# A fused state-space convolution and gated linear unit: kept weights, smaller transform units, one DMA per token load or store, and a spectrum swap by DMA

## The chip, the cores and the metric

The kernel runs on one core of a Trainium2 chip. The metric is device microseconds (us) of one execution, as the median of several. Executions of one kernel mostly agree within 1 to 1.5%; the kernel before had one outlier of 512.8 us, which no ratio uses. "Span" is the time from the first to the last instruction of the profiled execution and is about 2 us shorter than the time of that same execution.

The profiled execution is a single one. For the kernel before it took 281.01 us, 3.6 above the median; in the profiles of b_2q and b_one_stores, which change its stores alone, PE ends at 264.5 and 265.0 us where the profile of before has 266.8. So some 2 us of what this profile loses probably belong to that execution, and a difference of 2 us between two profiles is not safe by itself.

The engines, as the profile names them: PE (matrix multiplies) with PEld (its weight loads), DVE (vector engine), ACT (scalar engine), POOL, and SP, which here only issues DMA transfers. ACT issues some too (four of the token loads of before stand in its queue on the page). The order of each engine's instructions is fixed when the kernel is built. PSUM is where the kernel's matrix multiplies write; an evacuation is a copy of a result out of it, by ACT or DVE (1.01 and 1.22 us for one of 128x1024, on the page of before), and PE's next work in that slot stands behind it.

## The reference

Two branches are added to a residual. Sequence 2048, width 640, hidden width 1728; everything is bf16.

```python
def conv(q, k, v, shift_k, ssm_k, ssm_D):
    kv = shift4(k, shift_k) * v                    # four-tap shift along the sequence
    y  = irfft(rfft(pad(kv)) * rfft(pad(ssm_k)))   # long convolution, length 4096
    return q * (y[:2048] + kv * ssm_D)

def glu(x, w_gate, w_up, w_down):
    return (sigmoid(x @ w_gate) * (x @ w_up)) @ w_down

# The residual stream is q; glu runs on its layernorm. Output: 1 x 2048 x 640.
```

## The kernel before

The kernel computes both branches side by side. The gated linear unit runs over four blocks of 512 tokens: gate and up products, sigmoid times up, then the down product. The convolution runs in ten sub-blocks (five for each half of the channels). A sub-block has a first transform, a second transform, complex products on DVE, and a third transform; each half ends with a fourth transform. PSUM slots called "g" serve the linear unit, and two slots "c" the convolution. A table of numbers in the source fixes the order of all pieces of work on all engines. It was computed offline, so nothing moves when a transfer comes late.

The parts that the change touches, as they were:

```python
# token row = (n q m): partition p = 32*q + n, 16 tokens m for each partition
xq4 = A_q.flatten_outer_dims().rearrange("(n q m) d -> q n m d", q=4, m=NQ)
oq4 = out.flatten_outer_dims().rearrange("(n q m) d -> q n m d", q=4, m=NQ)

def load_x(q, m0, m1, eng, pri):                      # called for q = 0, 1, 2, 3
    dma(lambda e: e.dma_start(acc[32 * q:32 * q + 32, m0:m1, :], xq4[q][:, m0:m1, :]), ...)

def store(m0, m1, pri, two=False):                    # 8:12, 0:8, 12:14, 14, 15
    for q in range(4):
        dma(lambda e, q=q: e.dma_start(oq4[q][:, m0:m1, :], acc[32 * q:32 * q + 32, m0:m1, :]), ...,
            q="ACT" if two and q % 2 else "SP", ...)

# second transform: two units of 64 matmuls, each filling both "c" slots
for i in range(2):
    ...
    pe(1060, 64, f, ..., alloc=[(c, "c") for c in cs] ...)

# products of a sub-block: four multiplies of 64 partitions, then two of 128
for h in range(2):
    for b in range(2):
        a, o = slice(64 * h, 64 * h + 64), slice(64 - 64 * h, 128 - 64 * h)
        dve(..., nc.vector.tensor_tensor(Q(b)[a], X(b)[a], H(b)[o], ALU.mult), ...)
for b in range(2):
    dve(..., nc.vector.tensor_tensor(X(b), X(b), H(b), ALU.mult), ...)

# gate and up: sigmoid on ACT, product with the up half straight from PSUM on DVE
act(512, lambda: nc.scalar.activation(tl[sg][:], tl[cs[0]][:], ACT.Sigmoid), ...)
dve(512, 1, lambda: nc.vector.tensor_tensor(hT[:, fc, :], tl[sg][:], tl[cs[1]][:], ALU.mult), ...)
```

## Time and profile before

| | before |
|---|---|
| timed median | 277.43 us (first three runs), 276.8 to 278.0 us in the later sessions |
| profiled span | 279.1 us |
| PE busy / DVE / ACT | 252.7 / 207.0 / 144.0 us |
| PE's last work ends | 266.8 us |
| tail behind it | 12.3 us |

How to read it: the first line of the page gives each engine's busy time. The rows of 40 digits are slices of the span in tenths busy; PEclk is the granted clock in tenths. The chain is the sequence of work that ended last, followed backwards. The prediction below shows these lines for the kernel before.

### The profile page before, as it was taken

Reading aid. Unit: us, or ns where it says so; the run is one execution under the profiler, and the core shown is the slowest. Engines: PE = TensorE matmul, PEld = TensorE weight load, DVE = VectorE, ACT = ScalarE, POOL = GpSimd, SP = SyncE. Lnnn points to the kernel's source line nnn. Section 1 sums busy time; section 2 is a strip of 40 time slices with the busy share of each in tenths; the row PEclk is TensorE's granted clock in tenths of the full one; section 3 lists DMA queues with packets and bytes.
Section 4 is the critical chain, followed back from the end, with each engine's and each line's share of the span. In section 5 each row is a group of like instructions: output and inputs, shape, how many; then the busy total and the mean of one; then the engine's idle time right before and its main releaser. Section 6 shows DMA issues by size and latency. Waiting matters only on the chain.

```text
span 279.1 us, 9682 instructions
## 1 busy us (share of the span) xinstructions
PE 252.7 (91%) x4344; PEld 156.5 (56%) x4380; DVE 207.0 (74%) x342; ACT 144.0 (52%) x214; POOL 0.7 (0%) x6
## 2 busy tenths in 40 slices
PE   8899887997799999999999999999999999999800
PEld 3754334774355547777456646667655555776500
DVE  5433147899489998869979998999888568864840
ACT  4642586133699979436557654224457754341100
POOL 1000000000000000000000000000000000000000
PEclk9999997999799999999999999999999999999965
DMA  7999999999769984999987602900464110000266
GB/s 181 265 234 290 193 202 192 152 273 256 148 132 338 193 218 115 166 216 152 250 168 209 162 2 67 295 25 5 116 194 167 44 31 2 2 2 2 63 132 188
DMA packets 94720, 42.17 MB, mean 151 GB/s; under 512 B 68432, under 2 KB 93592, under 8 KB 94360
## 3 DMA queue, kind: packets, MB, share of 16 engines
q1 hardware_dynamic: 94488, 41.24, 65.5%
q8 instruction: 34, 0.56, 0.9%
q10 hardware_dynamic: 192, 0.33, 0.4%
q14 instruction: 6, 0.05, 0.1%
HBM read 35.00 MB, written 5.24 MB: 144 GB/s over the span
## 4 chain that ended last, share of the span: by engine, by line
PE 83%; issue 4%; ACT 3%; DMA 3%; DVE 2%; SPq 1%; DVEq 0%; ACTq 0%
PE g L730 34%; PE g L745 23%; PE c L514 8%; PE c L582 4%; PE c L493 3%; PE c L552 3%; PE c L551 3%; DMA acc<-in_A_q_dram 3%; PE g L775 2%; PE g L710 2%; ACT jk L615 1%; ACT jk L621 1%; ACT xnT L312 1%; SPq L366 0%; DVE xq L652 0%
## 5 line engine op out<-in xcount | busy, mean ns | idle before, releaser
L730 PE MATMUL g<-xnT,w 128*128 128x512 bf16 x484 | 116.3, 384 | 4.6 <-issue 2.1
L730 PEld LDWEIGHTS <-w 128*128 128x128 bf16 x520 | 48.5, 99 | 56.8 <-issue 3.3
L745 PE MATMUL g<-wd,hT 128*128 128x320 bf16 x448 | 67.7, 304 | 0.1
L698 DVE TENSOR_TENSOR hT<-sig,g 128x512 bf16<-128x512 bf16 x52 | 35.4, 687 | 25.8 <-PE g L730 17.8
L745 PEld LDWEIGHTS <-hT 128*128 128x128 bf16 x448 | 42.4, 99 | 17.3 <-issue 0.4
L696 ACT ACTIVATE sig<-g 128x512 bf16<-128x512 f32 x52 | 30.8, 596 | 27.8 <-PE g L730 26.1
L312 ACT CAST S<-c 128x1024 bf16<-128x1024 f32 x25 | 24.8, 1012 | 21.8 <-PE c L514 21.8
L536 DVE TENSOR_TENSOR P<-S 64x1024 bf16<-64x1024 bf16 x40 | 27.4, 686 | 8.2 <-PE c L552 3.7
L514 PEld LDWEIGHTS <-Mt 64*128 64x128 f16 x1280 | 19.9, 95 | 10.5 <-issue 9.3
L312 ACT CAST V<-c 128x1024 bf16<-128x1024 f32 x20 | 19.4, 1013 | 11.5 <-PE c L552 11.5
L514 PE MATMUL c<-T,Mt 64*128 64x64 bf16 x1280 | 22.3, 190 | 2.9 <-issue 2.9
L313 DVE CAST S<-c 128x1024 bf16<-128x1024 f32 x15 | 18.3, 1223 | 5.5 <-PE c L514 5.4
L315 ACT ACTIVATE T<-c 128x1024 bf16<-128x1024 f32 x14 | 13.9, 1022 | 15.6 <-PE c L493 15.6
L551 PE MATMUL c<-At,S 128*128 128x128 f16 x160 | 19.3, 219 | 0.0
L552 PE MATMUL c<-At,P 128*128 128x128 f16 x160 | 19.3, 219 | 0.0
L312 ACT CAST T<-c 128x1024 bf16<-128x1024 f32 x14 | 13.8, 1014 | 10.6 <-PE c L493 10.5
L551 PEld LDWEIGHTS <-S 128*128 128x128 bf16 x160 | 15.6, 98 | 1.3 <-DVE S L539 0.2
L552 PEld LDWEIGHTS <-P 128*128 128x128 bf16 x160 | 15.6, 98 | 1.2
L756 DVE TENSOR_TENSOR acc<-g,acc 128x320 bf16<-128x320 f32 x32 | 14.5, 485 | 0.9 <-PE g L745 0.7
L458 DVE TENSOR_TENSOR tb<-kt,sT 128x1024 bf16<-128x1024 bf16 x20 | 13.7, 687 | 0.7 <-ACT kt L312 0.6
L463 DVE TENSOR_TENSOR ta<-ta,tb 128x1024 bf16<-128x1024 bf16 x20 | 13.8, 688 | 0.3
L539 DVE TENSOR_TENSOR S<-S 128x1024 bf16<-128x1024 bf16 x20 | 13.1, 688 | 0.3
(76 smaller groups left out, 196.1 us busy)
## 6 DMA issues: line engine op xcount, KB each, us to landing
w<-in_B_w_gate_dram SPq DMA_DIRECT2D x11, 640.0 KB, 4.8
w<-in_B_w_up_dram SPq DMA_DIRECT2D x11, 640.0 KB, 6.8
kt<-in_A_k_dram SPq DMA_DIRECT2D x8, 320.0 KB, 7.6
vt<-in_A_v_dram SPq DMA_DIRECT2D x8, 320.0 KB, 7.1
xnd<-xq SPq DMA_DIRECT2D x4, 640.0 KB, 7.5
ht<-in_A_ssm_k_dram SPq DMA_DIRECT2D x16, 96.0 KB, 6.3
wd<-in_B_w_down_dram SPq DMA_DIRECT2D x3, 480.0 KB, 5.5
acc<-in_A_q_dram SPq DMA_DIRECT2D x4, 320.0 KB, 7.3
```

The costliest lines, as they stand in the source:

```text
L312: fa = lambda: nc.scalar.copy(out=out_fn(), in_=in_fn())
L313: fd = lambda: nc.vector.tensor_copy(out_fn(), in_fn())
L315: fa = lambda: nc.scalar.activation(out_fn(), in_fn(), ACT.Copy, scale=scale)
L514: nc.tensor.matmul(tl[cs[e]][:, b, 64 * kk:64 * kk + 64], lhsT=Mb[rows, k, 64 - 64 * r:192 - 64 * r], rhs=tl[T][rows, 2 * k + r].rearrange ...
L536: dve(n, 2, lambda a=a, o=o, b=b: nc.vector.tensor_tensor(Q(b)[a], X(b)[a], H(b)[o], ALU.mult), r=sr + ([(Z, b, 0)] if h else []), w=[(Z, ...
L551: nc.tensor.matmul(o, lhsT=tl[S_][:, b, 0, j, :], rhs=Ab[:, 0, :], start=True, stop=False)
L552: nc.tensor.matmul(o, lhsT=tl[Z][:, b, j, :], rhs=Ab[:, 1, :], start=False, stop=True)
L696: act(512, lambda: nc.scalar.activation(tl[sg][:], tl[cs[0]][:], ACT.Sigmoid), r=[(cs[0],)], w=[(sg,)], alloc=[(sg, "sig")], pri=pri - 2000)
L698: dve(512, 1, lambda: nc.vector.tensor_tensor(hT[:, fc, :], tl[sg][:], tl[cs[1]][:], ALU.mult), r=[(cs[1],), (sg,)], w=[(hk, fc)], pri=pri ...
L730: nc.tensor.matmul(tl[c][:], lhsT=tl[wb][:, k, o:o + P], rhs=tl[X][:, k, :], start=(k == 0), stop=(k == NC - 1))
L745: nc.tensor.matmul(tl[pd[i]][:, 0:320], lhsT=hT[:, fc, t4 * P:(t4 + 1) * P], rhs=wd[:, fc, 320 * i:320 * i + 320], start=(fc == 0), stop=( ...
L756: dve(320, 1, lambda i=i, m=m, pd=pd: nc.vector.tensor_tensor(acc[:, m, 320 * i:320 * i + 320], tl[pd[i]][:, 0:320], acc[:, m, 320 * i:320 ...
```

## The change

The intent is to move less (block 1 uses the weights of block 0, of which four tiles wait in the buffer that the convolution's V needs only later), to need fewer slots at once in the second transform, to issue fewer transfers, to take work off DVE, and to fill the end with matmuls that need no transform. The order table was computed anew.

```diff
-    def load_x(q, m0, m1, eng, pri):
-        dma(lambda e: e.dma_start(acc[32 * q:32 * q + 32, m0:m1, :], xq4[q][:, m0:m1, :]), ...)
+    def load_x(m0, m1, eng, pri):
+        dma(lambda e: e.dma_start(acc[:, m0:m1, :], xq4[:, :, m0:m1, :]), ...)
+    def weight(tr, n):
+        tr = 0 if tr == 1 else tr
+        if tr == 0 and n < 4:
+            return ("wv", n), lambda: tl["wv"][:, n]        # "wv" lies in V's buffer
...
-    def store(m0, m1, pri, two=False):
-        for q in range(4):
-            dma(lambda e, q=q: e.dma_start(oq4[q][:, m0:m1, :], acc[32 * q:32 * q + 32, m0:m1, :]), ...)
+    def store(m0, m1, pri, d0=0, d1=DM):
+        dma(lambda e: e.dma_start(oq4[:, :, m0:m1, d0:d1], acc[:, m0:m1, d0:d1]), ...)
...
-        for i in range(2):                                   # second transform
-            pe(1060, 64, f, ..., alloc=[(c, "c") for c in cs] ...)
+        for i in range(4):
+            pe(455, 32, f, ..., alloc=[(c, "c")] ...)
...
+        if idx in PRM["SWAP"]:                               # sub-blocks 5 to 9
+            for h in range(2):
+                dma(... tl[Z][a] <- tl[S_][o, :, 1] ...)     # swap of the halves by DMA
+            for b in range(2):
+                dve(... tensor_tensor(Q(b), X(b), Q(b), ALU.mult) ...)
...
+        elif fc in PRM["UP"] and PRM["UP0"] <= pri < PRM["UP1"]:   # 18 of 52
+            ev(512, lambda: hT[:, fc, :], lambda: tl[cs[1]][:], ...)           # ACT copies the up half
+            dve(512, 2, ... tensor_tensor(hT[:, fc, :], tl[sg][:], hT[:, fc, :], ALU.mult) ...)
...
-    for q in range(2):
-        load_x(q, 0, 1, "SP", FIX)
-        load_x(q + 2, 0, 1, "ACT", FIX)
...
+    load_x(0, 1, "SP", FIX)
+    load_x(1, 4, "ACT", FIX)
...
-    store(15, 16, 248.0)
+    store(15, 16, 247.0, d1=320)
+    store(15, 16, 248.0, d0=320)
```

(Cut: the down product of the last token tile goes half by half, the last two tiles come after the convolution, a table has a plane more that nothing reads, and the order tables are new.)

## The prediction

Passages are cut where marked. That a token DMA would move on four engines was an assumption; the trace before shows the 22 missing increments. The sum of +4.8 is 3.5 + 1.2 - 3.6 + 2 + 8 - 4.5 + 0.5 - 2.3. The term of +2, for the filter and D loads, is cut, and the terms still printed come to +2.8.

> **What bounds the kernel now.** I read the page from its top: engines first, then the slices, then the chain that ended last, then the chain in order of time, the waits and windows of the tensor engine and the timeline of the store queue. The timed median is 277.43 us; the profiled execution spans 279.1, so I work in the span and take off 1.7 at the end.
>
> ```profile
> PE 252.7 (91%) x4344; PEld 156.5 (56%) x4380; DVE 207.0 (74%) x342; ACT 144.0 (52%) x214; POOL 0.7 (0%) x6
> PE   8899887997799999999999999999999999999800
> PEclk9999997999799999999999999999999999999965
> DMA  7999999999769984999987602900464110000266
> PE 83%; issue 4%; ACT 3%; DMA 3%; DVE 2%; SPq 1%; DVEq 0%; ACTq 0%
> ```
>
> PE is busy for 91% and holds 83% of the chain. The slices say where it isn't full: 7 to 14 (45 to 75 us or so, where the DMA row is at 9 and the clock twice at 7) and the last two, where only stores run.
>
> ```profile
> 71.53 7.03 PE g L730 x24
> 262.06 1.14 PE c L582 x127
> 264.81 1.32 issue
> 266.92 0.84 DVE vt L313
> ...
> 268.70 0.82 DVE acc L591
> ```
>
> From the chain in order of time: PE ends at 266.9, DVE follows until 269.5, and stores fill the rest to 279.1. So the span is **PE's end plus a tail of 12.3 us**. The tail's cause is the store queue, which needed 16.29 us to issue twenty stores (timeline of SP):
>
> ```profile
> 259.35 16.29 SPq L598 DMA_DIRECT2D out_dram<-acc  x20
> ```
>
> PE's sum of work at the rates of undisturbed stretches of the chain: gate/up L730 520 x 0.2165 = 112.6; down L745 448 x 0.1365 = 61.2; second transform L514 1280 x 1.04/64 = 20.8; third 320 x 0.0555 = 17.8; first and last 9.6 + 9.9; warm-up 6.7; first eighty 4.6; the rest 3. Sum 246. So **20.8 us are lost before PE's end**: start and startup 2.1; 14.7 to 45.4 us 4.3; low clock after that 1.9; 64 to 82 us 5.1; some 5 in small switches between groups until 262; last transform 2.3. The views for the large ones:
>
> ```profile
> PE g L674 <- ACT xq L654: 1.6, 1, 1.6
> PE c L514 <- issue: 2.9, 1, 2.9
> PE c L582 <- issue: 1.3, 1, 1.3
> 40.00:50.00 10.00, 7.67 (x80) 4.76 (x80) 7.46 (x22) 5.67 (x10) 0.00 (x0) 0.83 1.11 173
> 70.00:80.00 10.00, 8.63 (x62) 3.90 (x64) 5.50 (x10) 7.46 (x14) 0.00 (x0) 0.83 0.53 99
> ```
>
> (The windows' last three columns are clock, DMA share, GB/s.) The first wait is block 1's normalisation, which waits for token tiles 4 to 7: their loads hold the chain for 7.83 us from 23.62. The second is a hole in the middle of 64 equal matmuls with no releaser. After each the clock is 0.83 over the window, and 24 L730 take 7.03 instead of 5.2.
>
> [...] 148 DMAs should leave 2368 completion increments, and 2346 are recorded; the 22 missing are 11 each on the two small loads (D and the shift filter) whose outermost dimension is 4. No duration before tests it. [...] Here 512 columns with PSUM take 687 ns and 1024 from SBUF 687.
>
> **The change, part by part.**
>
> *Kept weights.* Seven weight loads of block 1 go, 7 x 640 KB of 41 MB, in 45 to 90 us, where the DMA share is above 1. That should take the 2.9 us hole and its cold stretch (1.8) away, and 0.8 of weight waits: up to -4.5. The V buffer is not needed for the convolution until much later.
>
> *Second transform in single slots.* Matmul count unchanged; gate/down segments rise from 70 to 76 in PE's order. At about 0.08 us a switch: +0.5. It lets PE give way sooner; no lasting evacuation wait in the page is large enough to repay more.
>
> *DVE relief.* In five of ten sub-blocks four 64-partition multiplies (4 x 686) become two of 128 (2 x 687): 5 x 1.37 = 6.8 us. Eighteen up-halves go to ACT (+10.8) and come back as SBUF multiplies (DVE -5). DVE 207 to about 193, ACT 144 to about 156: neither was the bound, so 0 on the path directly.
>
> *Tail order.* 68 down matmuls, 9.3 us, now follow the last transform matmul. They cover its evacuations, the 0.8 and 1.3 waits there, and most of the last residual adds: -2.3 in front of PE's end, and DVE's work behind PE falls from 2.6 to about 0.6.
>
> *Token DMAs.* Twenty issues at the end become six, worth several us by themselves. But each old DMA had 32 partitions outermost [...]; the new one has DRAM shape 4 x 32 x run against 128 partitions[...]. In the packet records an engine moves 1280 B in 55 ns, 3840 in 149, 5120 in 196, 10240 in 385: 26 GB/s. Each of four engines gets 32 runs: tile 0 1.8 us, tiles 1 to 3 4.8, 4 to 7 6.3, 8 to 15 12.3. Estimates in order of time:
> - Start: tile 0 and tiles 1 to 3 come from two queues over the same engines, landing near 9 instead of 3.3 and 5.6: +3.5. Block 0's own small waits: +1.2.
> - Block 1's tokens are issued early and cost less than now: its normalisation wait and cold stretch go: -3.6.
> - [...]
> - Tiles 8 to 15 land at about 82 instead of 63, and six square passes of ACT stand before other evacuations in its order: +8 (4 to 11).
> - Kept weights -4.5, switches +0.5, last transform -2.3.
>
> Sum +4.8: PE's end at **271.7**; with the ends of these terms 266 to 277; I take 273.
>
> Stores: the big one (tiles 0 to 7) is issuable 6.6 us before PE's end and starts about 5 before; 12.3 on four engines, then 3.4 (12:14), 1.8 (14), and 2 x 1.0 (15), in line: -5 + 12.3 + 3.4 + 1.8 + 2 = 14.5, and 1.5 for issue and the end: **tail 16** instead of 12.3. Span 273 + 16 = 289, timed **287**.
>
> **The rivals.**
>
> *A. As above: four engines a token DMA.* For it: [...]the 22 missing increments. Against it: no duration; the fraction of these loads that hides is my guess. Time 282 to 292.
>
> *B. The new DMAs spread over all engines* (by how the compiler shapes them). Then every part gains. Block 0 with its down part ends near 59 instead of 64; the remaining PE work is about 191, switches 5.8, misses 1.5: PE's end 257.3. The tail is 0.6 (DVE) + 0.5 (issue) + 3.5 (landing and end, as from the last issue at 275.6 to 279.1): 4.6. Span 262, timed 260. For it: the issue time really is what fills the tail now, and it goes.[...]
>
> *C. Four engines, but loads mostly hidden.* ACT's early passes don't hold PE, and the start costs 2. PE's end is 262 to 265, the tail 14 to 16: timed 274 to 279, within 2%. For it: token loads are early in the queue and PE has transform work to put in front. Against it: every engine's order is fixed when the kernel is built, so a late pass holds what stands behind it.
>
> *D. The swap by DMA becomes a wait.* The last two sub-blocks leave about 6.8 and 10.6 us for swaps that I estimate at 6.3 and 9.2. If late, PE waits 0 to 3 us before the third transform. It adds to A or B, and decides nothing alone. ACT or DVE as a new bound (156 and 193 against PE's 252.7) I hold unlikely.
>
> **Range and chances.** A gets 0.6, B 0.2, C 0.2 (mostly within 2%, which is 271.9 to 283.0). Centre 287; the low end must reach into B with D on top, 264; the high end is A with all its terms late, 296. Faster by over 2%: 0.23; within: 0.16; slower: 0.61.
>
> **What would show it.** Right: fewer than 16 increments, and packets piled on few engines, for token DMAs; issue to landing of the 8:16 load and the 0:8 store over 12 us; first ACT statistics after 8 us; a PE wait on ACT at 60 to 85 us; the last store landing 14 to 17 us after PE's end; no unexplained hole at 68 us; DVE 190 to 196. Wrong: a 0:8 store that lands within 5 us and a tail below 7 us (B), or PE ending before 265 with a long tail (C), or PE's waits before the third transform above 3 us (D). Should DVE or ACT top the chain, my reading of the bound was wrong.

## More of the kernel before

One more view is needed later. It is the window of PE, PEld, DVE, ACT and POOL busy time (with instruction counts), then clock, DMA share and GB/s, of the kernel before at 80 to 90 us:

```profile
80.00:90.00 10.00, 9.79 (x163) 5.32 (x164) 9.91 (x16) 9.87 (x22) 0.00 (x0) 1.00 1.05 313
```

## The result, and the profile after

The changed kernel took **310.63 us** (309.82 to 311.25) against 277.62 us of the kernel before on the same chip (this median counts the outlier; it is 277.43 without): ratio 1.1197, 95% interval 1.1155 to 1.124. The direction was as predicted. The time lies outside the range of 264 to 296. A ratio here and below is the mean time of one kernel's fast runs over that of the other's fast runs of the same rounds, so it is not quite the ratio of the medians. Executions over 1.5% slower than the fastest of the same kernel are left out of the means.

The page of the changed kernel, the lines that answer to those shown of before (engines, slices, chain by engine):

```profile
PE 259.7 (84%) x4380; PEld 158.5 (51%) x4380; DVE 191.2 (62%) x331; ACT 155.0 (50%) x233; POOL 0.7 (0%) x6
PE   8099999999509999989799999999999999989000
PEclk9759999999957999999999999999999999999855
DMA  5695999983378008999995080963508360111221
PE 51%; SPq 20%; DVE 11%; DMA 8%; ACT 2%; issue 1%
```

DVE and ACT are where the prediction put them (190 to 196, about 156); the eighteen multiplies of copied up halves take DVE 423 ns each, those straight from PSUM 684, and a copy takes ACT 588. PE has two gaps that were not there (slice 2, and slices 11 and 12), and the empty stretch at the end is three slices long. SP's queue and DMA now hold 28% of the chain.

The chain in order of time (start, length, what):

```profile
62.97 24.92 DMA acc<-in_A_q_dram
...
277.34 9.36 PE g L780 x68
286.72 0.49 DVE acc L792
```

PE ends at 286.7 instead of 266.8. The matmuls put at the end fill 9.36 us and DVE is done 0.5 us later, but the span ends only at 309.5. The tail (what follows PE's end) is 22.8 us with six stores, where it was 12.3 us with twenty. In SP's timeline the six stand in one stretch:

```profile
265.64 35.88 SPq L623 DMA_DIRECT2D out_dram<-acc  x6
```

The waits (who waited for whom: us in all, times, longest) and the window that the kernel before spent with PE full:

```profile
ACT jk L639 <- DMA acc<-in_A_q_dram: 23.2, 3, 13.0
PE g L762 <- ACT hT L315: 12.0, 1, 12.0
PE c L698 <- DVE xq L676: 7.1, 1, 7.1
PE c L574 <- DVE S L555: 3.0, 3, 1.6
```

```profile
80.00:90.00 10.00, 1.54 (x8) 0.59 (x6) 1.28 (x3) 2.03 (x5) 0.00 (x0) 0.83 0.44 97
```

ACT stands 13 us in front of the statistics of tiles 8 to 15, whose load lands at 87.9 us. Behind it in ACT's order are the evacuations that free PSUM for PE, so PE does next to nothing from 80 to 90 us, and the clock falls to 0.83.

**Where the time went, as a ledger.** To compare kernels with different orders I gave each of PE's 4380 matmuls its undisturbed cost, the same in all kernels: gate/up 216.5 ns, down 136.5, second transform 16.25, third 55.5, fourth 9.7, first 10.6 or 19.4, warm-up 213, the small rest 57 to 150. Summed in the order in which their weight loads start, this gives 244.3 us of work. "Lost" at some sum of work is the time of that moment less the sum. The columns a_split_all and s_start_2q are experiments told below.

| work done | before | changed | a_split_all | s_start_2q |
|---|---|---|---|---|
| 10 us | 3.8 | 13.5 | 9.4 | 6.5 |
| 60 us | 13.7 | 14.6 | 10.2 | 7.3 |
| 70 us | 14.8 | 28.5 | 10.6 | 7.8 |
| 200 us | 18.8 | 39.7 | 22.2 | 19.2 |
| all | 22.2 | 42.0 | 24.1 | 20.9 |
| tail behind PE | 12.3 | 22.8 | 7.9 | 5.0 |

The changed kernel loses 9.7 us more at the start, gains 8.7 between 10 and 60 us of work, loses 12.7 more at tiles 8 to 15 (work 60 to 70), 7.2 more from there to 200, and gains 1.2 at the end: 19.7 up to the last weight load, 19.9 up to PE's end. With 10.5 more of tail this is the 30.4 us between the two spans. (The medians lie 33.0 apart, because the profiled execution of before was a long one.)

**The token transfers in the packet records.** Packets of 10,240 bytes are tiles 8 to 15 coming in, and tiles 0 to 7 going out:

| | first start to last end | mean time of one | in flight on average |
|---|---|---|---|
| load, before | 61.1 to 67.6: 6.5 us | 699 ns | 13.8 |
| load, changed | 66.0 to 87.3: 21.3 us | 646 ns | 3.9 |
| store, before | 269.4 to 275.6: 6.3 us | 725 ns | 14.7 |
| store, changed | 281.0 to 301.3: 20.3 us | 567 ns | 3.6 |

(128 packets each; "in flight" is the sum of their times over the stretch.) The completion increments tell the DMAs apart. Of before, 2346 are recorded for 148 DMAs: 16 for each of 146, and five for each of two small ones. At 16 each the 123 DMAs of the changed kernel would leave 1968, and 1836 are recorded. The 132 that are missing are 11 for each of twelve DMAs: the two small ones of before, and the ten token DMAs. The runs below bear this out: with the token DMAs in four (a_split_all) 22 are missing, and with the loads, the stores or one load single (a_split_stores, a_split_loads, l_late) 66, 88 and 33: 11 for each single one and for the two small ones. And from 283 to 297 us of the changed kernel, when no packets but the large store's are recorded, the DMA share is 0.25 of 16 engines. So four engines for this store is what the trace shows; that the other token DMAs have four each is read from the same 11 missing increments and, for the loads, from 3.4 to 3.9 packets in flight (tiles 0 to 3 together, 4 to 7, 8 to 15).

What makes a packet slow is another matter. Between 281 and 297 us of the changed kernel no packet but those of the large store is recorded, and still the ones that start from 281 to 283 took 760 ns on average, those from 289 to 295 some 395 to 413, and those from 295 to 297 1139 (a_split_loads shows the same course). So other traffic of this core is not what made the packets of the store slow; the cause stays open.

### The profile page after: what moved, and what is told of

Its sections match the earlier page's. It is cut to its first block, busy times and chain, and to the rows that moved or that the text cites. A ratio compares the mean times of both kernels' runs of the same rounds, so it can differ in the third digit from the quotient of the medians.

```text
span 309.5 us, 9677 instructions
## 1 busy us (share of the span) xinstructions
PE 259.7 (84%) x4380; PEld 158.5 (51%) x4380; DVE 191.2 (62%) x331; ACT 155.0 (50%) x233; POOL 0.7 (0%) x6
## 4 chain that ended last, share of the span: by engine, by line
PE 51%; SPq 20%; DVE 11%; DMA 8%; ACT 2%; issue 1%
PE g L762 22%; PE g L780 13%; DMA acc<-in_A_q_dram 8%; PE c L522 6%; SPq L444 4%; DVE P L552 4%; SPq L375 3%; PE c L606 3%; SPq L433 3%; PE c L574 3%; PE c L576 3%; SPq L422 2%; SPq L411 2%; PE c L502 2%; ACT jk L639 2%
## 5 line engine op out<-in xcount | busy, mean ns | idle before, releaser
L762 PE MATMUL g<-xnT,w 128*128 128x512 bf16 x380 | 89.5, 380 | 0.2 <-DVE hT L728 0.2
L780 PE MATMUL g<-wd,hT 128*128 128x320 bf16 x448 | 65.4, 300 | 0.0
L762 PEld LDWEIGHTS <-w 128*128 128x128 bf16 x380 | 34.2, 98 | 37.0 <-issue 0.4
L762 PE MATMUL g<-xnT,V 128*128 128x512 bf16 x140 | 33.0, 389 | 12.0 <-ACT hT L315 12.0
L728 DVE TENSOR_TENSOR hT<-sig,g 128x512 bf16<-128x512 bf16 x34 | 23.1, 684 | 21.0 <-ACT sig L726 10.5
L315 ACT CAST S<-c 128x1024 bf16<-128x1024 f32 x30 | 29.8, 1014 | 7.4 <-PE c L522 7.2
L762 PEld LDWEIGHTS <-V 128*128 128x128 bf16 x140 | 13.3, 99 | 27.8 <-issue 13.4
L723 DVE TENSOR_TENSOR hT<-sig,hT 128x512 bf16<-128x512 bf16 x18 | 7.6, 423 | 24.7 <-ACT sig L720 12.8
L574 PE MATMUL c<-At,S 128*128 128x128 f16 x160 | 19.2, 219 | 3.0 <-DVE S L555 3.0
L639 ACT ACTIVATE jk<-acc 128x640 bf16<-128x640 bf16 x13 | 9.6, 736 | 23.4 <-DMA acc<-in_A_q_dram 23.2
L576 PE MATMUL c<-At,P 128*128 128x128 f16 x160 | 19.2, 219 | 0.0
L316 DVE CAST S<-c 128x1024 bf16<-128x1024 f32 x10 | 12.2, 1222 | 9.1 <-PE c L522 9.1
```

What stands on the lines that cost most here:

```text
L315: fa = lambda: nc.scalar.copy(out=out_fn(), in_=in_fn())
L574: nc.tensor.matmul(o, lhsT=tl[S_][:, b, 0, j, :], rhs=Ab[:, 2 if zc else 0, :], start=True, stop=zc)
L576: nc.tensor.matmul(o, lhsT=tl[Z][:, b, j, :], rhs=Ab[:, 1, :], start=False, stop=True)
L639: plan.op({"ACT": (0.75, lambda m=m: nc.scalar.activation(jk[:], acc[:, m, :], ACT.Identity, accum_out=st[:, TMP, m:m + 1]))}, r=[("acc", ...
L762: nc.tensor.matmul(tl[c][:], lhsT=w()[:, k, o:o + P], rhs=tl[X][:, k, :], start=(k == 0), stop=(k == NC - 1))
L780: nc.tensor.matmul(tl[pd[i]][:, 0:320], lhsT=hT[:, fc, t4 * P:(t4 + 1) * P], rhs=wd[:, fc, 320 * i:320 * i + 320], start=(fc == 0), stop=( ...
```

## The experiments

Seventeen kernels ran. All passed the comparison with the reference; w_lessdve computes something else and passed it too, so its result isn't to be relied on. Times are medians; the ratio is against the kernel before on the same chip in the same rounds, and is what to compare across sessions. Its 95% interval is some 0.3 to 0.7% to each side. (In l_late's ratio the two slow executions are counted.)

| run | time, us | ratio |
|---|---|---|
| a_split_all | 278.62 | 1.005 |
| a_split_loads | 293.05 | 1.058 |
| a_split_stores | 295.30 | 1.066 |
| b_one_stores | 291.74 | 1.053 |
| l_late | 286.13 | 1.037 |
| l_early | 282.78 | 1.023 |
| s_start | 274.57 | 0.990 |
| s_start_2q | 271.66 | 0.982 |
| b_2q | 276.29 | 0.995 |
| s_noup | 281.01 | 1.012 |
| s_noswap | 278.21 | 1.002 |
| b_switch | 281.33 | 1.014 |
| s_spread | 278.08 | 1.007 |
| w_lessdve | 269.73 | 0.972 |
| s_evac | 271.58 | 0.978 |
| y_traffic | 272.88 | 0.983 |
| s_late3 | 279.93 | 1.005 |

### The token DMAs: a_split_all, a_split_loads, a_split_stores, b_one_stores

The theory was that four engines a token DMA make the whole loss, and the rival that the new order is worse in itself. a_split_all cuts each token load and store of the changed kernel into four again, in the same places; the next two do so for loads alone and for stores alone.

```diff
-        dma(lambda e: e.dma_start(acc[:, m0:m1, :], xq4[:, :, m0:m1, :]), ...)
+        def four(e):
+            for q in range(4):
+                e.dma_start(acc[32 * q:32 * q + 32, m0:m1, :], xq4[q][:, m0:m1, :])
+        dma(four, ...)
```

(The stores in the same way.) b_one_stores is the converse: the kernel before, with each of its five stores in one DMA. (In its file the four pieces stay in the order table; the first to run issues the whole store, the others nothing.)

```diff
-        for q in range(4):
-            dma(lambda e, q=q: e.dma_start(oq4[q][:, m0:m1, :], acc[32 * q:32 * q + 32, m0:m1, :]), ...)
+        dma(lambda e: e.dma_start(oq4[:, :, m0:m1, :], acc[:, m0:m1, :]), ...)
```

> The changed kernel with every token load and store cut again into four DMAs of 32 partitions, in the same places of the same queues; all else of the change stays. Four-engine theory: the whole loss is the token DMAs, so this shows the rest of the change alone: tensor engine done near 257 to 260, tail 7 to 9, timed 262 to 270 (faster than before by 3 to 6%). Rival, the new order itself is worse (spectrum swap, ACT's longer list, single-slot transform): it stays above the kernel before, 278 to 300, with the waits of 110 to 160 us still there.

> Only the token loads are cut into four; the stores stay single. Four-engine theory: the wait of ACT for tiles 8 to 15 (23 us) and the late start go, the tensor engine ends at 257 to 262, and the tail stays long, about 18 to 23 us: timed 276 to 283. Rival (loads matter little, the order does): 295 to 308.

> Only the stores are cut into four; the loads stay single. Four-engine theory: the tensor engine still ends near 287, the tail falls from 22.8 to 7 to 10 us: timed 293 to 298. Rival (the tail is bound by something else, say the memory side): within 3 us of the changed kernel's 310.

> The kernel before with one thing of the change: each store one DMA over 128 partitions. Four-engine theory: after the last add at 269.5, tiles 0 to 7 (12 to 20 us) and 8 to 11 (6 to 8 us) go out one after another over four engines: timed 288 to 298. Rival, the issue of twenty stores is what fills the tail: 271 to 275, faster.

Measured: 278.62, 293.05, 295.30 and 291.74 us. Single stores cost 293.05 - 278.62 = **14.4 us** in the changed kernel and 291.74 - 277.08 = **14.7 us** in the kernel before, against the same stores in four. Single loads cost 295.30 - 278.62 = **16.7 us**. Together with what a_split_all has over the kernel before (1.5 us) that is 32.6, and the change cost 33.0. b_one_stores settles the tail by itself: five issues in place of twenty made the kernel slower by 5%. The rival "issue fills the tail" falls.

The first run missed what the four-engine theory asked for, though: the remainder of the change brings nothing, where I had expected 262 to 270. 278.62 is at the lower edge of the rival's range (278 to 300), and waits of the kind that it named, at 110 to 160 us, are still there. So both were right in part: the token DMAs make nearly the whole loss against the kernel before, and the new order eats what the rest of the change wins. a_split_loads missed its 276 to 283 for the same reason. The page and the waits of a_split_all:

```profile
PE 254.5 (92%) x4338; PEld 157.4 (57%) x4380; DVE 191.1 (69%) x331; ACT 155.1 (56%) x233; POOL 0.7 (0%) x6
```

```profile
PE c L577 <- DVE S L558: 3.0, 3, 1.5
PE c L704 <- DVE xq L682: 2.8, 2, 2.5
```

(The second and third lines are PE's longest waits.) DVE is relieved, the end is shorter (tail 7.9 us), and yet PE's end is 2 us later than in the profile of before (4 later than in b_2q's). By the ledger it loses 5.6 us more at the start, wins 9.1 between 10 and 60 us of work, and gives 7.7 back from 70 to 200. PE's wait of 12.0 us for ACT is gone, and its wait at the start (the lower of the two) is 2.5 us instead of 7.1. The three waits for the products before the third transform (the upper) stood in the changed kernel too, also with 3.0 us. The start and the stretch from 70 us of work on are the two questions that follow.

### Which load, and how: l_late and l_early

Both have the stores in four. In l_late only tiles 8 to 15 come in one DMA, in l_early only tiles 0 to 7.

```diff
+        if m0 == 8:      # l_late;  l_early: if m0 < 8
+            dma(lambda e: e.dma_start(acc[:, m0:m1, :], xq4[:, :, m0:m1, :]), ...)
+            return
```

> The changed kernel with all stores and the loads of tiles 0 to 7 in four DMAs; only the load of tiles 8 to 15 is single. With loads single the kernel took 295.3, with all in four 278.6: 16.7 us to be shared out. Theory of two parts: the four engines alone make this load land some 12 to 16 us later (about 75 instead of 61.6 us), ACT waits 4 to 8 us for it and the time is 283 to 288; the rest of the wait comes from the queue that the earlier single loads hold up. Rival, this one load is all of it: 291 to 295.

> The converse: only the loads of tiles 0 to 7 are single, tiles 8 to 15 and the stores are in four. Theory of two parts: the start is 4 us late, and as the SP queue is held up behind the four engines' backlog, tiles 8 to 15 are issued 8 to 11 us later but move in 6 us: ACT waits 0 to 4 us; 282 to 287. Rival, early loads cost only their own landing: 279 to 280.

Measured: 286.13 (281.75, 285.12, 287.13 and 288.13, the last two slow; the profile is the fastest) and 282.78 us. Over a_split_all l_early costs 4.2 us. l_late costs 3.1 and 6.5 in its two fast executions, 9.5 in the slowest. So together they come to 7 to 11 us from the fast executions (13.7 with the slowest) of the 16.7: the two do more harm together. What spreads l_late's executions I haven't traced. ACT's waits for the tokens in l_late, and those in l_early:

```profile
ACT jk L650 <- DMA acc<-in_A_q_dram: 2.7, 1, 2.7
```

```profile
ACT jk L650 <- DMA acc<-in_A_q_dram: 10.8, 2, 8.1
```

In l_early, tiles 8 to 15 come in four DMAs, and move in 7.4 us. But SP issues them at 61.7 us in place of 51.9 in a_split_all, so they land at 71.8 and ACT waits 8 us for them, more than the 0 to 4 expected. PE hardly felt it (0.5 us), so nearly all that l_early costs lies at the start. The early single loads hold up SP's queue for everything behind them. A weight load that stands behind them shows it, in SP's timeline of the changed kernel:

```profile
4.06 5.03 SPq L375 DMA_DIRECT2D V<-in_B_w_gate_dram  x1
```

and the same issue in a_split_all:

```profile
3.79 0.52 SPq L378 DMA_DIRECT2D V<-in_B_w_gate_dram  x1
```

So the changed kernel got tiles 8 to 15 late in two ways: issued 11 us later (63.0 against 51.9), and moving for 21.3 us instead of 6.5. In l_late the same four-engine load took 17.9 us, with a median of 393 ns a packet. The DMA share over it was 0.35, and 0.34 in the changed kernel, so here too it isn't the amount of other traffic that tells the two apart.

### The start and the end: s_start, s_start_2q, b_2q

a_split_all issues tiles 1 to 3 from ACT's queue alone. s_start issues tiles 0 to 3 as the kernel before did. s_start_2q adds that two of each four stores are issued by ACT. b_2q does only the latter, to the kernel before.

```diff
+    def first_x(e):                               # s_start: ahead of the weights
+        for m0, m1 in ((0, 1), (1, 4)):
+            for q in range(4):
+                (nc.sync if q < 2 else nc.scalar).dma_start(acc[32 * q:32 * q + 32, m0:m1, :], xq4[q][:, m0:m1, :])
...
-                e.dma_start(oq4[q][:, m0:m1, d0:d1], ...)
+                (nc.sync if q < 2 else nc.scalar).dma_start(oq4[q][:, m0:m1, d0:d1], ...)     # s_start_2q
...
-    def store(m0, m1, pri, two=False):            # b_2q, in the kernel before
+    def store(m0, m1, pri, two=True):
```

> From the version with all token DMAs in four: tiles 0 to 3 are issued as in the kernel before, half of the partitions from each queue and all ahead of the weights. Theory, the 5.6 us that this version loses at the start against the kernel before come from tiles 1 to 3 standing alone in ACT's queue beside the weights (landed 7.8 against 4.9 us): first transpose near 9 instead of 12 us, time 3 to 4 us lower, 274 to 276. Rival, the start is late by DVE's and ACT's order of the statistics: less than 1.5 us.

> From the version with tokens 0 to 3 issued as before (274.6 us): each store's four DMAs go two to SP's queue and two to ACT's. The tail there is 8 us behind the tensor engine with 24 issues from one queue in 26 us. Theory that issue still sets the tail: 1 to 2.5 us less, 272 to 273.6. Rival, the landing of the last piece sets it: within 0.7 us.

> The kernel before with one edit: of each four store DMAs two are issued by ACT, two by SP. If the issue of twenty stores from one queue sets its tail (12.3 us behind the tensor engine): 3 to 5 us faster, 272 to 275, and then the rest of the change is worth about nothing. If the last large store (tiles 0 to 7, issued only after the last add, 6.3 us of packets on all engines) sets it: 0 to 1.5 us faster, 275.5 to 277, and 4 to 5 us of the best version's gain belong to the new order of the tail.

Measured: 274.57, **271.66** and 276.29 us. The start was worth 4.0 us, as expected: three of the 5.6 us that a_split_all loses there come from the queue. Two store queues were worth 2.9 us in the new order by the medians and 2.0 by the ratios (0.990 and 0.982, whose intervals just touch; the runs are of two sessions), so about what was expected, and 1.5 us in the kernel before. There, tiles 0 to 7 can't go out before the last add behind PE, and their 128 packets then take 6.2 us (264.9 to 271.1), 14.8 in flight, whoever issues them. In the new order the large store runs beside PE's last 9.4 us, and only the small stores of the last tiles are left behind: the tail is 5.0 us. s_start_2q beats both kernels: 1.8% under the kernel before (ratio 0.9791 to 0.9855).

### What is lost from 70 us of work on: s_noup, s_noswap, s_spread, w_lessdve, s_evac, b_switch, s_late3

This stretch is 80 to 150 us or so in time. The theories, one after another: ACT's copies of the up halves (s_noup takes them out), the swap (s_noswap), ACT's row of six statistics passes (s_spread starts them earlier and scatters them), DVE's amount of work (w_lessdve leaves 13.7 us of it out; s_evac gives seven evacuations to ACT), more visits (b_switch makes twenty more of them in the kernel before; a visit is one run of partial-height matmuls, those that use 32 or 64 of the 128 rows, between full-height ones), and the place of the third transform (s_late3).

```diff
-            ev(512, lambda: hT[:, fc, :], lambda: tl[cs[1]][:], ...)                         # s_noup, on a_split_all
-            dve(512, 2, lambda: nc.vector.tensor_tensor(hT[:, fc, :], tl[sg][:], hT[:, fc, :], ALU.mult), ...)
+            dve(512, 1, lambda: nc.vector.tensor_tensor(hT[:, fc, :], tl[sg][:], tl[cs[1]][:], ALU.mult), ...)
             # (and a multiply is pulled forward where its PSUM slot is needed)
...
-               SWAP=(5, 6, 7, 8, 9), ...                                                     # s_noswap, on a_split_all
+               SWAP=(), ...
```

> From the version with all token DMAs in four (278.6 us): the eighteen up-halves are again multiplied straight from PSUM by DVE, without ACT's copy. That version's tensor engine loses 4.0 us in three waits for products (114 to 147 us) that the kernel before hasn't. Theory that ACT is too full at 70 to 100 us (9.8 to 10.0 of 10 us in its windows) because of the copies: those waits fall below 1.5 us and the time falls by 2 to 4 us. Rival, DVE is the late one there: the waits grow and the time rises by 1 to 5 us. Copies off the path: within 1 us.

> From the version with all token DMAs in four: the spectrum swap by DMA is undone in its five sub-blocks, DVE multiplies 64 partitions at a time again (DVE +6.8 us, ten DMAs fewer). As the product waits lie before the sub-blocks that swap, I expect the swap to be off the path: within 1.5 us of 278.6. Rival, the swap gives DVE the room that the second half needs: 2 to 6 us slower. Rival, the swap's latency costs: 1 to 3 us faster.

s_noup took 281.01 us, 2.4 more than a_split_all (1.9 by the ratios, whose intervals overlap): its product waits grew from 3.0 us in three to 3.2 in five, and two waits of PE for hT came, 2.4 us. So nothing speaks for the copies as the cause, and the hT waits say that they help a little. s_noswap took 278.21, no difference: the swap is off the path in both ways, though it takes 7.8 us off DVE (198.9 against 191.1).

```diff
+        # s_spread, on s_start_2q: the seventeen passes for tiles 8 to 15 in ACT's order
+            if x is before[0]:
+                out += [rest.pop(0) for _ in range(3)]      # three ahead of the fifth piece before
+                going = True
+            out.append(x)
+            if going and rest and x.on == "ACT":
+                out.append(rest.pop(0))                      # then one behind each of ACT's pieces
```

> From the version with two store queues: ACT's seventeen passes for the statistics of tiles 8 to 15 start in ACT's idle stretch before 62 us, three at once and then one after each other piece of ACT's work, in place of six in a row at 67 to 72 us and the rest behind them. Theory that this burst holds ACT's evacuations, makes DVE late and so the products late (4 us of waits for them, and most of the 8 us that this version loses on the tensor engine between 85 and 150 us against 1.5 in the kernel before): 2 to 5 us less than that version. Rival, DVE's own work is what is late there: within 1 us.

s_spread took 278.08, 6.4 slower. The tokens landed at 65.5 us (62.4 in s_start_2q), after I had put passes that need them ahead of the first sigmoid:

```profile
66.58 0.74 ACT L683 ACTIVATE jk<-acc 128x640 bf16<-128x640 bf16 x1 [13.37 <-DMA acc<-in_A_q_dram]
```

PE waited 6.0 us for that sigmoid. That part is my edit's own fault. But from 70 to 130 us of work it lost 9.1 us, and s_start_2q 8.4, although no six passes stood in a row any more. So, as far as this run can tell, the row of passes isn't the cause either.

```diff
-            dve(1024, 2, lambda: nc...                                                        # w_lessdve: t1, t2 of sub-blocks 1 to 5
+            dve(1024, 2, lambda: None if 1 <= idx <= 5 and c in (t1, t2) else nc...
...
-    ... 213, ... 244, 266, 302, 314, ... 332, ... 317, ...                                    # s_evac: out of ON_DVE
```

> From the version with split token DMAs, the old start and two store queues (271.7 us). Wrong result on purpose: in sub-blocks 1 to 5 two of the four shift products and their two additions are left out, 4 x 0.69 = 2.7 us of DVE work for each sub-block, 13.7 in all; everything else stands in the same order. Theory that DVE is the bound of the stretch from 85 to 150 us: the waits for products (4 us) go and the tensor engine's loss there falls from 8.6 to below 4 us, so 4 to 6 us faster, 265.5 to 268. Rival, the loss is in the order itself (more visits to partial-height matmuls, slots): within 1.5 us.

> From the same version: seven evacuations of the convolution that DVE does between 100 and 145 us (1.22 us each, 8.5 in all) go to ACT, which is 35 to 70% busy there. Result right. If DVE is the bound of that stretch: 1.5 to 4 us faster, 268 to 270. If the order is: 0 to 2 us slower, as ACT's row gets longer.

w_lessdve took 269.73 and s_evac 271.58, by the ratios 1.0% and 0.4% less than s_start_2q (the second is within noise). Both missed what the theory asked for. Of the 7.7 us lost between 80 and 130 us of work, 5.8 stay when DVE has 13.7 us less to do. DVE's amount of work is a quarter of it.

```diff
+            o.halves[0]()                    # b_switch, in the kernel before: 32 of the 64 matmuls,
+            x = next(...)                    # the next gate, up or down group of PE's order,
+            x.engs["PE"][1]()
+            o.halves[1]()                    # and the other 32
```

> The kernel before with one cost doubled up: each of the twenty runs of 64 second-transform matmuls is opened in the middle by the gate, up or down group that follows it, so that its runs of partial-height matmuls rise from 53 to 73 with no work added. From the trace a visit costs about 0.43 us (0.30 going in, 0.13 coming out): 8 to 9 us slower, 284 to 287. Rival, my first figure of 0.08 us a switch: 1 to 2 us slower. Rival, the wait is hidden by what comes next: nothing.

b_switch took 281.33, 4.5 us more by the medians and 3.8 by the ratio (1.8 to 5.8) for twenty more visits: 0.23 or 0.19 each, with an interval of 0.09 to 0.29. The ledger says the same: between 70 and 200 us of work it has 13 visits more than the kernel before and loses 7.2 us there instead of 4.0, so 0.25 each. The expectation of 0.43 was too much, because weight loads start ahead of their matmuls (by 27 ns in the second transform and 134 in the down product, medians of the kernel before) and I had counted that lead; the 0.08 that the prediction used is just below the interval. s_start_2q makes 45 visits in that stretch of work and the kernel before 34: 11 x 0.25 = 2.8 us, an estimate of the visits' share in what the new order loses there.

What the trace of s_start_2q shows at the largest of the three waits is DVE idle in front of products that PE then waits for (start, length, line, operation, tiles, and in brackets what it was idle for):

```profile
124.63 1.23 DVE L316 CAST S<-c 128x1024 bf16<-128x1024 f32 x1 [3.14 <-PE c L525]
127.04 0.49 DVE L798 TENSOR_TENSOR acc<-g,acc 128x320 bf16<-128x320 f32 x1 [1.18 <-PE g L786]
127.56 2.83 DVE L555 TENSOR_TENSOR P<-S 64x1024 bf16<-64x1024 bf16 x4
130.42 1.29 DVE L558 TENSOR_TENSOR S<-S 128x1024 bf16<-128x1024 bf16 x2
```

The second transform of that sub-block ends at 126.0, the products at 131.7, and the order gives PE 3.4 us of other work in between. The theory from this was that the third transform stands too early; s_late3 moves it behind one or two more groups.

```diff
+            x = next((o for o in order[i + 1:] if o.on == "PE" and o not in pair), None)   # s_late3, on s_start_2q
+            ours = set(pair) | set(self.v3[k])                                             # third transform and its evacuations
+            new = order[:i] + [o for o in order[i:j + 1] if o not in ours] + [o for o in order[i:j + 1] if o in ours] + order[j + 1:]
```

> From the version with split token DMAs, the old start and two store queues (271.7 us): in sub-blocks 0 to 4 the third transform moves behind one or two more groups of the tensor engine's work (1 to 4 us later), nothing else. Theory that the place in the order makes the waits for products (3.0 us in three waits, and more in small ones): they fall below 1 us and the time by 2 to 3.5 us, 268 to 269.7. Rival, the waits only move to the next user of the same slots: within 0.8 us.

s_late3 took 279.93, slower than s_start_2q by 8.3 us as the medians stand and by 6.2 by the ratios (1.005 and 0.982; another chip and session). Its waits:

```profile
PE g L809 <- DVE acc L839: 2.5, 1, 2.5
PE c L544 <- ACT V L354: 2.4, 5, 0.7
...
PE g L827 <- DVE acc L839: 1.3, 1, 1.3
PE c L650 <- ACT V L354: 1.1, 1, 1.1
```

No wait for products is left, and more than their 3.0 us came back as waits for PSUM: for the "c" slots that the third transform now held longer, and for a "g" slot. So the waits moved, as the rival had it, but they also grew, which neither expectation had. **What stays open:** what a better order of this stretch would be, and how the rest of the loss divides. Of the 7.4 us that s_start_2q loses there beyond the kernel before, the runs show that the swap isn't a part, that taking out the copies, the row of passes or seven evacuations on DVE doesn't win it back, that about 2 us hang on DVE's work, and that moving the third transform alone doesn't repair it. The visits' share of some 3 us is the estimate above. That the slots and the order bind each other there is how I read it, not something that a run isolates.

### The hole at 68 us: y_traffic

The prediction gave the kept weights 4.5 us, from a hole of 2.9 us in the middle of 64 equal matmuls. y_traffic puts the seven reads of weights back into s_start_2q. They are copies within DRAM to a place that nobody uses, where the removed loads wrote to the on-chip buffer: as many bytes read, but not quite the same traffic.

```diff
+    idle = dr.tile([7, P, NC, 512], BF16, name="idle")
+    def extra(n0, n1):
+        for n in range(n0, n1):
+            nc.sync.dma_start(idle[n], (wgr, wur)[n % 2][:, :, 512 * (n // 3):512 * (n // 3) + 512])
```

> From the same version: the seven weight tiles of block 1 are read again (7 x 640 KB) into memory that nothing uses, four just behind the load of tiles 8 to 15 and three behind a table at about 63 us, so that only the traffic of the loads that the change removed is back. Theory that this traffic made the hole and waits of the kernel before at 60 to 82 us: 2 to 5 us slower, with a hole in the tensor engine or a late token tile. Rival, transfers are hidden there: within 1 us.

Measured: 272.88, ratio 0.983 against 0.982 of s_start_2q: nothing beyond noise, and no hole. From 60 to 70 us its DMA share is 1.07 at 313 GB/s, more than the kernel before had there (1.05, 285 GB/s):

```profile
60.00:70.00 10.00, 10.00 (x115) 4.75 (x115) 9.79 (x16) 6.64 (x14) 0.00 (x0) 1.00 1.07 313
```

So in the new order the reads of the weights are hidden. The hole itself is a habit of the old order: it is in b_one_stores at the same place, and smaller in b_switch, where the same runs of small matmuls are cut in two:

```profile
PE c L514 <- issue: 2.7, 1, 2.7
```

```profile
PE c L537 <- issue: 1.6, 1, 1.6
```

In the kernel before the hole lasts from 68.25 to 71.16, and one of the 34 packets of the queue that the page calls "instruction", 16 KiB, is moved from 68.7 to 69.7. That PE waited for it was not shown. Full DMA engines alone don't bring the hole on: the new order, in which such dense runs are shorter, hasn't got it even with the traffic back. That the spacing is what removed it is argued from these kernels, not isolated.

## Why the prediction was right or wrong

- **The mechanism was right.** Four engines a token DMA (rival A, given 0.6): twelve DMAs with 11 increments missing, 3.6 and 3.9 packets in flight in the two large ones, a DMA share of 0.25 while the large store was alone, and splitting them all brings the time from 310.63 to 278.62 (the parts by themselves are 16.7 and 14.4). Rival B (all engines) and rival C (mostly hidden) are out. The chance of 0.61 on "slower" went to the right side.
- **The size was wrong, and the first mis-sized term is the packet.** The prediction took "10240 in 385" ns, the time of the fastest packet, for both large transfers. In the load it was 646 on average and in the store 567. "12.3" became 21.3 and 20.3 us. The warning was in the records of before: the same packets had means of 699 and 725 ns there. I put that down to all engines working at once and expected it to go with four. It didn't go, not even where the store had the engines to itself.
- **"Tiles 8 to 15 land at about 82 ... +8 (4 to 11)"**: they landed at 87.9, and the ledger shows +12.7. (The "instead of 63" was a misreading: before, their last packet ends at 67.6.) Against a_split_all (61.6) that is 26 us late, 15 by moving slowly and 11 by a term that the sum did not have: the early loads hold up SP's queue, and the load is issued that much later.
- **"tail 16"**: it was 22.8. The large store started 5.7 us before PE's end, as foreseen, but took 20.3 us instead of 12.3; the small stores behind it took less than foreseen.
- **"Start ... +3.5" and block 0's "+1.2"**: +9.7. Of this, single DMAs are 4.1 (13.5 against 9.4), and the queue that tiles 1 to 3 were put into 2.9 (9.4 against 6.5 in s_start_2q). I had read the second from the diff and not counted it. The other 2.7 (6.5 against 3.8) I have not traced. Tile 0 and tiles 1 to 3 came from two queues, and their 256 packets, from 2.2 to 11.9 us, had 3.9 in flight together, as many as one large token DMA alone: as I read it, they shared its engines.
- **The gains between 10 and 60 us of work** were -3.6, +2 (the cut term, which no run measured) and -4.5, in sum -6.1; measured -8.7. The sum was near, but one cause wasn't: putting the reads of the kept weights back did nothing (y_traffic).
- **"Second transform in single slots ... +0.5"** and "DVE relief ... 0": from 70 to 200 us of work the new order loses 7.2 us more. The visits are some 2.8 of them by estimate (11 more at 0.25 us, not 6 at 0.08). The rest lies in the new order, in part in products that come late for its third transforms (3.0 us in three waits), and the prediction didn't look for it: it took PE's small losses of before as a property of PE and not of the old order. Rival D, the swap as a wait, is not it: those waits lie before the sub-blocks that swap.
- **Last transform -2.3**: -1.2 measured, and a tail of 5.0 us once the stores are spread. Rival B's 4.6 for it was right, its 262 was not: PE's end was put at 257.3, and is 265.6 in the best version.
- The first view was over-read in one thing: "the tail's cause is the store queue, which needed 16.29 us to issue twenty stores". b_2q and b_one_stores show that the data of the large store filled it. A queue that is busy in a timeline may be so with a single issue (the same one held SP's for 5.03 us in the changed kernel and for 0.52 in a_split_all). Two smaller slips: PE's slices that aren't full, at 45 to 75 us, are 7 to 11 and not 7 to 14; and the 1.7 us taken off between span and time came from one long execution (281.01 us, span 279.1), as the span is always the shorter of the two.

So the step that failed first is the cost of four engines, as a sum of the fastest packets: right in kind, and about 1.7 times too small for the two large transfers (12.3 us put, 21.3 and 20.3 measured). It isn't the whole of the miss. The span was put at 289 and was 309.5. Of these 20.5 us, the tail makes 6.8, tiles 8 to 15 make 4.7, the start makes 5.0, and the stretch from 70 to 200 us of work makes 6.7; the other terms give 2.7 back. The last two had other steps behind them: tiles 1 to 3 in ACT's queue alone, which the sum left out, and a new order that was taken to cost 0.5.

## What to carry to other kernels

Before you merge DMAs to save issues, find out what the merged one does by itself: here, with a dimension of 4 outermost, the large load and store had 3.9 and 3.6 packets in flight instead of 13.8 and 14.7 and took three times as long (21.3 and 20.3 us instead of 6.5 and 6.3), and single early loads delayed what stood behind them in the same queue (tiles 8 to 15 were issued 11 us later). Price a transfer by what packets of its size took on average in the trace, not by the fastest one. And when a change comes with a newly computed order, measure the order alone, with the rest undone: here, with the token DMAs in four, it came out 0.5% slower than the kernel before, and 7.6 us of what it won elsewhere were lost again from 70 to 200 us of work.
